# A gated recurrence and a spectral convolution on one core: odd batches walk the spectrum backwards, three kinds of operation may run on another engine, and the table of the order is new

## The chip, the core and the metric

The kernel runs on one core of a Trainium2 chip. The metric is the device time of one execution in microseconds (us). The median of three runs before the change is 484.12 us (484.09 to 484.51).

A core has engines that run side by side, each through its own list of instructions in order: TensorE (PE) multiplies matrices and writes them to PSUM; VectorE (DVE), ScalarE (ACT) and GpSimd (POOL) do elementwise work; SyncE (SP) here only issues DMAs, and all DMAs of this kernel are issued by it, in order. "PEld" in the profile is the load of a matmul's weights.

## What is computed

```python
# x, f_logit: (4, 6272, 256); B = 4 batches, S = 6272 steps, D = 256 channels
sig = 1.0 / (1.0 + np.exp(-f_logit))
f = lower_bound[None, None, :] + (1.0 - lower_bound[None, None, :]) * sig
i = 1.0 - f
for t in range(S):
    h = f[:, t] * h + i[:, t] * x[:, t]
    y[:, t] = h
...
proj = y @ w_proj                      # (4, 6272, 768) = x1, x2, x3
X2 = np.fft.rfft(x2, n=S, axis=1)
H = np.fft.rfft(filter_fft, n=S, axis=0)[None, :, :]
x2_conv = np.fft.irfft(X2 * H, n=S, axis=1)
out = (x1 * x2_conv * x3) @ w_out
```

The FFTs are done as products with matrices of cosines and sines. S is split as 128 x 49.

## The kernel before, in words

**Order.** Nothing of the order is decided while the kernel runs. The Python code first lists all operations with `op(kind, cost, fn, ...)`; `cost` names the engines on which an operation may run, with a price each that was used to make a plan, and `r` and `w` name what it reads and writes. `Plan.emit` (line 100) then issues them in the order of the string `ORDER` (line 117): three characters are 18 bits, the operation's number, its engine (ACT, DVE, PE, POOL or SP) and, for work in PSUM, the first of its banks. So the string fixes each engine's order, SyncE's DMAs among it, and the engine of each operation that has a choice. Many choices have `either` (line 282), ScalarE or VectorE.

**Stages.** `prepare` (line 395) makes the tables of cosines and sines and turns the filter once into its spectrum H, written to DRAM in 16 units of 8 pairs of channels. Then for each batch:
- `hgrn(b)` (line 299), 13 chunks of 512 steps: load f_logit into FL and x into XT (three buffers each, line 308); sigmoid (`sig`, ScalarE, line 311); the product of input and sigmoid (`u`, GpSimd, line 313); PE turns both (`su`, line 325); the gate's value (`f`, lines 338 and 340); VectorE's scan (line 346) writes h into HA; for the first 3072 steps a copy is wrapped behind the end of HA (`wrap`).
- `spectrum(b)` (line 764): `phase_p` multiplies h by the middle third of w_proj (`P`, line 673, 13 groups, cast to X2 by `x2`). Then for four groups of four units: `F1` (line 686) and its cast `A`; the small `mini` (line 702) with VectorE's `zm` (line 708). For each unit, `unit(b, u)` (line 717) loads the unit's part of H into one of three buffers Hu (`H`, line 721, one DMA of 392 KB), transforms (`F2`, line 731), has VectorE multiply by H (`prod`, line 744), and transforms back (`I2`, line 754, evicted to Th by `Th`).
- `gate(b)` (line 360), 13 chunks x 2 halves: x1 and x3 (`x13`, line 373) are evicted to x1s and x3s (`xs`), and their product goes to zt (`z`, GpSimd, line 389).
- `phase_o(b)` (line 774), 13 groups: the last inverse transform (`I1`, line 787), VectorE's product with zt (`y`, line 793), the projection with w_out (`proj`, line 805), the eviction into one of three osb buffers (`o`), and the store (line 815).

The order mixes these: hgrn of batch b+1 runs beside spectrum, gate and phase_o of batch b, and P of b+1 starts before phase_o of b is done. Copies go through a helper, so L270 and L272 are ScalarE's copies of many operations, L275 and L277 VectorE's, L280 GpSimd's; they are told apart by the tiles they write.

**Buffers of H.** Unit u of batch b takes the Hu buffer (16 b + u) modulo 3, whatever is in it; each of the 64 units has its own load, and a load waits until the products of the unit that held its buffer are done.

Of the kernel before, what the change touches and what calls it, by code (L numbers as in the profile page):

```python
# [58 lines left out]
class Plan:  # L59
# [58 lines left out]
    "A8gAAYBBgAOYABIAoQBLgACIBGgAmRBVgBQgAcSBagBfgAnTA7YAPIAyUBkgA9AAlVBpgBCAA+WBugBDQBAGAjSA/GBMYA6TBFABzgAgUBHY"  # L118
    "A5VBEIAQABNWERgA2SBPOA1TARIAvUBWAAYYB4gBIQAsVBRABXSADgAtUBOGBSUBYCAfWBbYESgBKAAxXArWBJABgYAeXBZCEdgBcQA3WBlA"
    "BTMBhSEpgApXBdIBqYBUEBmWATIBjCEegAUIBoGBvYBrUBeIBtEBiKAzQAFgBnGB0YBwQBsMAiSByABxIEqgB1WASAAGgAwTB5YETAB3OB9Y"  # L120
    "B6UA0SB2OAbQB7MAkRB8MCKSCIWAEYEUYCLCCBQEfACJOB/UAWICCICNSCAECEWCOKEVQCFGEgYEZUEWIAdSErAE1gAqTEXIE2gAhWEaECTS"
    "AIAAVYEbMEhWAHACDYElQAJAEsYEiOCUCCRUFBgEmAFCgEjOClSCSECQgCGgANACWUEnIE3ACMYEtWCVYCXEEuOExQE4YEvOFNgCmCCcUFOg"
    "EyACZgCaSCdMFDACjWEzIE5UCbCCkGE9SCeYE6MFEYALACfQFZgE+CE7MAuWFagAMACsWCPgAKACHgCgICuUCtGFPAFFWE/KFJQFGGFQYFjg"
    "CvEFHOCoSFkgFKAC3UChgCYgFbACpKA4WCnYFRWC4EFLIFcYCxSFSGFVUCyCFTOC1QFtgFugFWEC+SCqgEwYC2AFdWFXMCrgFlAE0YC6QCwY"
    "C5YC/CDAUC7IFmYFeGFgSDBEFfODJQFhCF3gC9gDHUDKAF4gFiKAXYFnWFvACigEcYDDQDCYFoODIEFqSFwYDEADSUFpOGBgGCgFrCDQQCzg"
    "DTEDMWC0gFsKDRADFgFMYFxUF5AC8gE8YDbQDNODLYFyEDZSDUYFAYDcADGgDVWFzMF6YDaCF0QDWGDiSF1IGLgDkUGMgDjKGDADeWEYYF2I"
    "DtSDlEDdYDYgGEYDfGDrUDOgF7QDsEDnWDuCF8IF+UDoGF9IEoYD0SGVgDmYF/EFYYD2WDqgDPgD1CDwQAaYGAMGWgD3GD/SDpgGNADxIGFW"
    "DhgDvYD5UGOYGGGEAKGIQD6EGHOD9SMVgGJADXgEIUD8gD+CEGWD4YGKIFIYEJEGPSEkYEHGGSUGXAGQKEBYECQEKYGTEMhgGYYGRKEPWD7g"
    "EDAAZYMWgMigGUMEQGGZSELQFUYGfgEFgGaCGcWJSUEEgGbKB+YGdGMXAJTVGeOJUMGgSEMAJVNGmWJWYGhCEOgDygGiUMtgMjAMugGsQDgg"
    "GnGGqSGtIDzgG0WGrCGwQHEgGjEENgGoSG1GGyUGpCGuWGzMGxAG2SGvGGkQG3KMvAG4UJXWGlAG5MJYXJcSJZGJdTJaHHLgG6QJfLG8UHSg"  # L130
    "JbYG7AJeKG+WJhTG9MG/GJgYHFQJiSJjDHHIHAWJkCJmUHBGHIIJlYJnVHMSJoEHCWJrQHPKHZgJpFJsRJtAJqYHiUJuBHOKJwQJxTJvYJyA"
    "J1RHDOHqgHjEJ2SJzLJ6QHGYJ3BHgWJ4KJ0YHJUHhGHTRHUYHKEHNYHkWJ5YHVJJ7TJ8AJ/UHlGHWJHQQJ9DHaVHRAKBMHxgJ+YHrSHcNKAX"
    "HmQHbYKCHMwYHdNHXUHnAKEXHYEHuKHeQH4gKGHIGUKDYHtKHfAHoWKFTIHEHyQHpOH/gKJSKHDH0IHsYIIUKLCKIYHvWIJEH1IH5SHzYHwG"
    "IKUH6YMYYH7KIQgH2QILEIAWH8KH3AIMUKKSINEICOIXgH9QKMCKOTIDOKPUH+AKNYKTVKQDIOQIegIRWKREIPIIBYKUSKVFKSYITOIsTKWC"
    "IEQItDIUOISYIYVIZYKXYIFAKYSIaNIlgKZUKaCKdTIuQIbNKfDKeXIvAIVSKbMI2gIfVKgHKcYIWCImQIiNKiUIcSIgYKkEKhYIhNKjXIdC"
    "KnWIpIKlHIjUI9gKpGKmYI3SIkEIoIIwWInYKoRIxGMkYI5KIqUJEgKqBKsQI6KKtWIrEI+RKvGMZUKrYJLgJAJKuAMdWMaEKxTKwYM5gMeG"
    "MbMKyQM6gKzDK2RK0AJBJIyTK4BK1YIzDMlQMfOK3VMcYMmAMpSK5FMnII0WMqCNFgMxUK6YNGgM7AI1OK7QMrKK8RI/YMyEI4YM1WM8YK+B"
    "MzMK9ANRgI7SM2GNSgLARI8CM3OLBQJGYJFULCBK/YLFSLDAJHMNHAM9WLEYNBQJIMM+GJCTNdgLHCNIYNegM/ONCALGVLKSNTANDIJMWLIF"
    "NUYJDDLLVJOONJQLMCLNFLPTJPONKANNUNfALJYNngNLINVWNogNOELQSLOYLRDNPMNZQNWGNgYRVTLSCNxgNXONaAJJUNygRXDRWSJKENbI"
    "LTYNhWRYCNkTNpANiOJNYJQQN8gNjONlDN7gNqYRaVJRARbSNmLRdCLUWRcFLZQLVONQYNrSNuUNsCLaILWWOFgNzAOGgNtKLbQNvEN0YLXG"  # L140
    "NwMLjSN9ALeWLYgLkKM0YLcAN1UN+YLfOLoSN2ELdgN4QN3MLgWN5AOPgOQgOHAMgYN6ILlULhGOIYLpKLtQLmELigN/WLuIOCSOAGLqUMsY"
    "OZgODCOBONMYOagLngNAYLyQLrEOEKNYYOJWORAOMULsgLzILvSUYgONEOSYOKGOOML0QObALwCOLOL3UMoAOcYLxgOTSM4YL4MOWWOUCL1A"
    "UkgOVKL8UPVgNEAOdQL2gOXGL9ML5SOeANcAOfIL+UL6COYOOgQL/EMGSL7gOhIUxgMBWOiIUwgMLUMCOUZgOvQMAgMHKPOgMDWOwAPHgOpS"
    "MEGOnQOqKOzWOoAO3SO0GOlQO4COtWOmAOrSOuOO5QOsCOxWO6IUyAO1SOyGMMMOjQO2CO7WMIUOkAO8OMNSUmAMJMMQQMOCO9WMRIO/UO+O"
    "RZYPBQPAEPDSPCIPIWReYPECPPUUaAPKOPFQRfSUzYRgTRhCPGIRkWRiDPLOPjQRmGPlSPkAPJYRlWRjYPSMPcgRpXRnGMFgPMQPmCPQYPRM"
    "RoYPWVRrHPdSPYNPtgPNARqUPXYRuXRsEPZNPTQRwHRtYPpUPUAPfKPnWP0gPeYPqEPaQUbYPgKPoGPuURvSP7gPbAPwMRzTUlgPrWRxCPhQ"
    "R1DPsOR0SPxMPvYP1TRyYR2CQJWPiAP4LQCgR4SQKGPyQP3LP8UR6CP9YP2YQLWPzAR3YP+MQTgP5SQMGQDQP/MP6CQNWR5UQGIQOGQagQAS"
    "R7ER9VQFIQUWQBCR8YR+RR/FQWOQhgQPSSABQEYSCUQQCSBYQHQQXOQbVQIAQRSSDXQogQdNSEESHQSFHSIRSJAQSKSGYUcUSKBQeNQvSUdE"
    "SMXQVYQwCQcYUeMQxQSLYQ5gSNWSOHQYSQyISPGQiUQZCSQYQzWQkMSRQQ0GSSRQlMQfSSUBQpWSTAQqYRAgQgCQ1USVYQsOUgQQ2ESWSQjY"
    "QrOU9gUnYUhASXTQmUSZDUiIRHgSYCQtWU8gQnEQ3SQ6QSaYQ4KQuGRBUQ8ISbSRCYScTSdCSgWRDMSeDShXSiGUoSSfYREMSjHSlQUpCSmU"  # L150
    "SkYQ9ISnASqWSoESrXQ7YRIUU+AUqKSpYROgQ+QMPgSsGStPU/YRFSQ/ARLMUsWRGCSvQVIgRKMUtGRPRVJgSxASuYSwVUuOS0TSyFS1QRJY"
    "S2DSzYU0URSJS3AS5WU1ES6XRQYRRJS4YS7GU4SS8HS+QVUgU2MS9YVKARTWVVgS/RRUGU5KRMUVLYTBJTAATDWRNEU6KVAQTEXVBATFOVEU"
    "TCYTGHVCITISVFEVhgVMWVggTHYVWAVGMMKgVQQTJTVNGVqgVXYTKKMSUTLDVOOVRATNSMTETOTTPCMUgTSUVSITMYTQDVYVVrgXRgTTXVZF"
    "TXSTRYTVPTUEVcQVaNViATWYZYXV0gZZUV1gVdAVjYZdVTYKZeWZaHZgGZfNTZSVsAVeITcWTaCTdOThQVtYZbEVkSTbgVnUTiIVlCTeWV+g"
    "VoEV/gVmKVuQTfGVpMTmSV2ATggVxWTnKWJgTjUVvAV3YWIgVyGVwITrSTkEVzOWAATlgV4QV7UV5ATsKWBYToWWSgUjAV8EV6ITtSTpGV9M"
    "T1QUvYTuCTqgTwWVPYWTgUfAT2IWCSTvgU3YVbAWFUU7YWDCTxOT3QWcgWKAWdgWEKTyWWGEWLYWUAWHMT6STzGT7KT/UVTYT4AWMWUAMWPS"
    "WVYWNGT5gT8QWQCT0gWOOUEUT9AWRKVHYWWWWeAVfYWZQWXGUFMWfYUBScogWaAVDYcbgUrAWYOXYgUGUUCCccgT+gWbIWgWWjScngWhGUHE"
    "czgWiOUDgUJQWkKUOWWlKUKIW+UXKgW4SW/EUPOW0Qc0gW5CULUW1AW8WcdAWoSW9OWyQWpCWsWUMEWwSWtOWzAW2UcpAWuQW3EcqYW6WWvA"
    "WmUW7OWxCWqQWnMUQWWrAUTSURGXAUUUKXCQZhYXBMXESXDAXGWZcYXFKXLUXHGXSQceYc1AXOMXISZiWZjXZkGXJKZnVZlHXVIXmSZpFXMY"
    "XoWXnCZmYZoVXNMZsRZqFcfSXTYZuBXUIZrYXfgcjUcgCZtRc/gXpGchKZxQXwgdAgckEZyWZvJcrSZzAclMZ0GXWQcsCZ1YXsWXXActKXgU"  # L160
    "ZwYXZQXtGXjMcvSXhYdBAXPWc2YXiMZ2VcwCXQGXcIZ3UX+gdLgZ4FXqWUIgcxKZ5EZ7RXrGZ8VZ6YaAUXbIaBSZ9BXkWXaYaDCZ+NX3gaCE"
    "XdQdMgXlGZ/YXuSX4UXvKXeAYOWX5YXxSdCYYPGYMQX0Kc3WYNAXzKaFTc4GaEYc7QaHDX6MYFgaGSc8AaKTaICX7MaLUaMDaJYaPSaNEaQT"
    "c9IdNAYWgX8UXyYdYgaOYdXgX9EaSLX1Qc5OaRCdOYX/TX2AaUVYBLaVSaWFYQWaXCYGQYCLaTYYRGYSSaZVYIIYTCYdgaYYaaWaeXabFafU"
    "YJIYHYacGdDSYAYc6YahEYUVajQdECYkgYVNadYakRagHdFKYKUdZAYDWYfYaiYamJalAYXSYEGaoRYZKanYYLEYyWapQYzGYaKYeUYYYatS"
    "arAYgMYbWYrgaqBavCY0QasYYhMYcGYlTauSY1AYmYYoLYiWY8gawCY2QYjGYtYYnLaxYYsUY3AaySYuMY4WZDgdaYa0CYpQUSgY5GUNgYvM"
    "Y9ScmAY6WazUZAKYqAZKga3Va1EYwQY7Oa2YZETY/KYxAdHWa5FY+Ya4QZHLZRgdIGZBRdkga6Aa8VdjgdJOZCBZMYa9Ua7YbBQa+FZLRZGL"
    "a/EZFYZSWbDAbAYbCVZOJfNgZITbEFbGQZNJbFYZJDbHVbLSbIAZVObMTZTYbJFdPQbNCbKYdTUZUObODbQXdQAdtgciYZPSbSHdugdRIbPY"
    "dlAUVWdUMZQCZWQdmYUWOcuAbRSdVMUXgdbWbTCZXAbVTdcOdfUbUYbXDbWSddOdgEd3ghbQd4gbYChcRdhMbaSbZYheBbfWhdAc+YbbKdvA"
    "dnUdqQdoEdwYbgOhgSeBgdrAhhTeCghiCdpMbcWd5AdsIhjDbkUd6YbdGdxSblMd0QdyCbegbhWdSAeLgdzKeMgd1Ad7UbiGd2IbpSeDAd+W"
    "bjgbqKbmQeWgd8EeEYeVgd/Gd9MbrSbnAeAObsCbuUbogcyYeFQfUgeNAbvMbzSeIWeOYb0KeJGefgbwUbtgeGAeKOb4SbxEeHIdWAePWdGA"  # L170
    "b1Ub5KeQGb9QeXAeROeSSb2EeYYb+Ib6WeTCb3gehAbygeUKdKAcCUeggb7GdeYeZQcDMdiYecSeaAb8gcHWedCebIb/UeeKcEQcAEeiYcIO"
    "cFAcMScBgejUcNKemQcJWenAekMcOSeoIcKGelMcRQcPCcWUe9WcXMcSIcQgepSfbge+GhkYezUeqKfBQexWhfYfCIevSeyGe7Qe0EetWe8A"
    "e3UeuGe5QewCe1We6Ae/Se4EerQfAKe2GhlUhmVesAhqWhoNhrXhnEhsOfDShtHhpYfFQfECfHUfGIfJWhuYfIEfOShvQfKGfRKhwRfVUhyB"
    "fQKfLWh0ThxAh1RhzYh2DfMOh5Qfigh3Bh6SfXMfpWh4Yh7Ah+TfqGfYMfrQfPYh/Uh8CfSWiALfzgiBEh9YiDVcGgfsAfcScLgfWYiEUfTG"
    "ffKiCYftQiGEfZWiFFfeKfjTfuAiHYiIVfmLf6gfaGiJSfdYfvQfkYiKFflLfgWfwAiNUfhOiOViLCgBgf0QiPEiMYiQFfxSiSWfyKgPUf2I"
# [11 lines left out]
def kernel(  # L187
# [79 lines left out]
    def copy(e, dst, src, scale=None):  # L267
# [5 lines left out]
        elif e == "DVE":  # L273
            if scale is None:
                nc.vector.tensor_copy(dst, src)  # L275
            else:
                nc.vector.tensor_scalar(dst, in0=src, scalar1=scale, scalar2=None,  # L277
                                        op0=AOP.mult)
        else:
            nc.gpsimd.tensor_copy(dst, src)  # L280

    def either(n, runs=1.0):

        return {"ACT": 0.045 + runs * n / 1200.0, "DVE": 0.07 + n / 960.0}
# [429 lines left out]

    def unit(b, u):
        ka = u % NA * UE
        k = (b * NU + u) % NP
        h = (b * NU + u) % NH  # L720
# [156 lines left out]
```

## Time and profile before

| what | value |
|---|---|
| median of three runs | 484.12 us |
| the profiled execution: time, span | 487.22 us, 485.2 us |
| mean granted clock of TensorE | 0.993 |
| busy: PE, ACT, DVE, POOL | 451.7, 423.0, 413.3, 299.6 us |
| moved by DMA | 116.49 MB, 240 GB/s on average |
| H loads (line 721) | 64 of 392 KB |
| z on POOL (line 389) | 104, 1214 ns each |
| u on POOL (line 313) | 52, 2247 ns each |
| H product on DVE (line 744) | 128, 1199 ns each |
| scan on DVE (line 346) | 104, 123.1 us in all |

The profiled execution has a span (first to last instruction) and a time that includes what lies around it. A row of the profile's groups reads: line, engine, operation, what is written <- what is read, shapes, count | busy us, mean ns of one | idle time of the engine just ahead of these instructions, and what ended that idle time. The chain of waits is followed back from the last instruction, at each step to what released it or to the instruction before it on its engine. In a timeline each row is a start, a length, an engine and an instruction; in SyncE's rows the length of a merged row includes what it waited for.

Batch 0's P begins at 77.5 us of the span, and P of batch 3 at 397.7 us; the four changes of stage are at about 77, 180, 290 and 398 us.

### The profile page before, as it was taken

What the parts mean: (1) busy time and instruction counts of PE and PEld (TensorE: products, weight loads), DVE (VectorE), ACT (ScalarE), POOL (GpSimd) and SP (SyncE); (2) the same over time, 40 slices, a digit from 0 to 9 for tenths busy, and PEclk for the clock granted to TensorE, in tenths of its full rate; (3) what the DMA queues carried; (4) which work ended last, traced back from release to release, by engine and by line L of the source; (5) the groups of instructions that cost most, each with busy time, mean ns of one, the idle gap of its engine ahead of it and who ended that gap; (6) DMA issues with size and microseconds to landing.
All of it is one profiled execution on the core that took longest, in us unless ns stands there. A gap on an engine that the chain in (4) does not pass through costs nothing.

```text
span 485.2 us, 14710 instructions
## 1 busy us (share of the span) xinstructions
PE 451.7 (93%) x6041; PEld 347.1 (72%) x6041; DVE 413.3 (85%) x446; ACT 423.0 (87%) x613; POOL 299.6 (62%) x313
## 2 busy tenths in 40 slices
PE   8988998999999989999998998989989899999995
PEld 7776777677667879767566888656757788676784
DVE  7788985899999985999999984979989984999773
ACT  6988999999998969989898978999979868999844
POOL 6775994486897910946896723878675522666600
PEclk9999999999999999999999999999999999999998
DMA  8989999545688994464879975475777861544177
GB/s 330 397 287 354 329 306 313 188 122 162 208 274 291 356 346 173 134 195 135 240 236 360 386 265 228 152 232 190 227 245 250 315 227 38 178 148 151 54 287 294
DMA packets 41731, 116.49 MB, mean 240 GB/s; under 512 B 4384, under 2 KB 6304, under 8 KB 41664
## 3 DMA queue, kind: packets, MB, share of 16 engines
q1 hardware_dynamic: 41664, 115.56, 70.0%
q8 instruction: 47, 0.77, 0.7%
q14 instruction: 20, 0.16, 0.1%
HBM read 84.54 MB, written 31.00 MB: 238 GB/s over the span
## 4 chain that ended last, share of the span: by engine, by line
PE 46%; DMA 17%; DVE 14%; ACT 10%; issue 5%; POOL 3%; SPq 1%; ACTq 0%; DVEq 0%; POOLq 0%
PE PS L373 11%; DMA out_dram<-osb 8%; PE PS L673 7%; DMA FL<-in_f_logit_dram 6%; PE PS L754 6%; DVE PP L744 5%; PE PS L805 5%; DVE HA L346 5%; PE PS L731 4%; PE PS L686 4%; PE PS L325 4%; DMA Hu<-H 2%; ACT osb L272 2%; ACT fTs L338 2%; PE PS L787 2%
## 5 line engine op out<-in xcount | busy, mean ns | idle before, releaser
L389 POOL TENSOR_TENSOR zt<-x1s,x3s 128x490 f16<-128x490 f32 (+1 forms) x104 | 125.3, 1214 | 94.5 <-ACT x3s L270 43.9
L744 DVE TENSOR_TENSOR PP<-PS,Hu 98x1008 f16<-98x1008 f32 x128 | 146.5, 1199 | 8.6 <-PE PS L731 3.3
L313 POOL TENSOR_TENSOR XT<-XT,FL 128x1024 f32<-128x1024 f32 (+1 forms) x52 | 116.8, 2247 | 47.5 <-ACT FL L311 18.6
L346 DVE TENSOR_TENSOR_SCAN HA<-fTs,HA,PS 128x512 f16<-128x512 f32 (+1 forms) x96 | 113.4, 1204 | 6.9 <-ACT fTs L338 5.9
L373 PE MATMUL PS<-HA,W 128*128 128x490 f16 (+1 forms) x416 | 105.5, 370 | 3.1 <-DVE PP L744 1.4
L793 DVE TENSOR_TENSOR ys<-PS,zt 128x1024 fp32r<-128x1024 f32 (+1 forms) x52 | 58.6, 1151 | 9.0 <-PE PS L787 3.6
L272 ACT ACTIVATE osb<-PS 128x1024 f32<-128x1024 f32 (+1 forms) x49 | 47.7, 988 | 19.6 <-PE PS L805 11.1
L338 ACT ACTIVATE fTs<-PS,nomc 128x512 f32<-128x512 f32 (+1 forms) x89 | 59.3, 680 | 4.6 <-PE PS L325 4.1
L270 ACT CAST HA<-PS 128x1024 f16<-128x1024 f32 x57 | 57.8, 1032 | 3.8 <-PE PS L686 3.3
L805 PE MATMUL PS<-Wo,ys 128*128 128x256 f32 x392 | 56.8, 291 | 3.2 <-ACT osb L272 1.7
L311 ACT ACTIVATE FL<-FL 128x1024 f32<-128x1024 f32 (+1 forms) x52 | 53.1, 1021 | 7.6 <-DMA FL<-in_f_logit_dram 7.4
L272 ACT ACTIVATE x1s<-PS 128x490 f32<-128x490 f32 (+1 forms) x95 | 56.0, 592 | 3.5 <-PE PS L373 1.3
L373 PEld LDWEIGHTS <-W 128*128 128x128 f16 x416 | 33.9, 98 | 33.7 <-issue 10.8
L754 PEld LDWEIGHTS <-PP 98*128 98x128 f16 x1024 | 49.5, 98 | 11.9 <-issue 3.3
L270 ACT COPY x3s<-PS 128x490 f32<-128x490 f32 (+1 forms) x90 | 51.8, 579 | 4.6 <-PE PS L373 3.1
L805 PEld LDWEIGHTS PS<-Wo,ys 128*128 128x128 f32 x392 | 49.0, 188 | 7.9 <-ACT osb L272 2.2
L325 PE MATMUL PS<-iden,FL 64*128 64x64 f32 x784 | 46.6, 233 | 7.8 <-ACT afs L270 2.1
L754 PE MATMUL PS<-VA,PP 98*128 98x98 f16 x512 | 51.8, 207 | 1.6 <-DVE HA L346 0.9
L270 ACT CAST Th<-PS 128x784 f16<-128x784 f32 x62 | 50.9, 830 | 1.4 <-PE PS L754 1.2
L325 PEld LDWEIGHTS PS<-iden,FL 64*128 64x128 f32 x784 | 34.0, 139 | 25.2 <-DVE HA L346 5.6
L754 PE MATMUL PS<-VB,PP 98*128 98x98 f16 x512 | 51.6, 207 | 0.0
L673 PE MATMUL PS<-W,HA 128*128 128x256 f16 x392 | 44.8, 273 | 3.4 <-ACT osb L272 3.4
(110 smaller groups left out, 677.9 us busy)
## 6 DMA issues: line engine op xcount, KB each, us to landing
Hu<-H SPq DMA_DIRECT2D x64, 392.0 KB
FL<-in_f_logit_dram SPq DMA_DIRECT2D x48, 512.0 KB
XT<-in_x_dram SPq DMA_DIRECT2D x48, 512.0 KB
out_dram<-osb SPq DMA_DIRECT2D x48, 512.0 KB
X<-in_moe_filter_fft_dram SPq DMA_DIRECT2D x9, 512.0 KB
H<-Hu SPq DMA_DIRECT2D x16, 196.0 KB
H<-Hu SPq DMA_DIRECT2D x16, 128.0 KB
Hu<-in_moe_filter_fft_dram SPq DMA_DIRECT2D x2, 512.0 KB
```

The source lines that it names most:

```text
L270: nc.scalar.copy(dst, src)
L272: nc.scalar.activation(dst, src, AF.Copy, scale=scale)
L313: op("u", {"POOL": 0.1 + 0.553 * nb}, lambda e, xt=xt, ft=ft: nc.gpsimd.tensor_tensor(xt, xt, ft, op=AOP.mult), r=[("ft", k)], w=[("xt", k)])
L325: nc.tensor.transpose(bank(pb)[:, at[p] + j:at[p] + hn:nb], src[ps, j, cols], iden[ps, ps])
L338: nc.scalar.activation(fT, sT, AF.Identity, scale=by, bias=1.0)
L346: nc.vector.tensor_tensor_scan(h, fT, bank(pb)[:, 512 - hn:512 + hn], init, op0=AOP.mult, op1=AOP.add),
L373: nc.tensor.matmul(PS[:, p, 0:n], W13[:, kh, js], HA[:, HB[kh] + t0:HB[kh] + t0 + n], start=(kh == 0), stop=(kh == 1))
L389: nc.gpsimd.tensor_tensor(late["zt"][:, jb, :, m0:m0 + nm], xs(0), xs(1), op=AOP.mult),
L673: nc.tensor.matmul(pp[:, r - r0, :], column(HB[kh], q_of(r)), W2[:, kh, :], start=(kh == 0), stop=(kh == 1))
L744: nc.vector.tensor_tensor(PP[:TB, k, o, :, :, 1:64], px.unsqueeze(1).broadcast_to([TB, 2, UE, 63]), hh[:, :, :, 1:64], op=AOP.mult)
L754: nc.tensor.matmul(PS[:, ib + o, pr * TB:(pr + 1) * TB], PP[:TB, k, o, n, 2 * pr:2 * pr + 2, :], v[:TB], start=(n == 0), stop=(n == 1))
L805: nc.tensor.matmul(po[:, i, :], late["ys"][:, yk, kh, i * 128:(i + 1) * 128], Wo[:, kh, :], start=(kh == 0), stop=(kh == 1))
```

## The change

- The 16 units of H are walked from 15 down to 0 in batches 1 and 3 (the groups of four backwards too), and from 0 up in 0 and 2.
- `unit` keeps a list of which unit each Hu buffer holds. If the unit that is due is held, no load is listed; otherwise the buffer used longest ago is loaded. The PP buffer is counted by order of use.
- `u`, `wrap` and `z` have VectorE as a further choice (`either_of`).
- `ORDER` is a new string, made for the new list of 2325 operations (2334 before).

```diff
+    def either_of(e):
+
+        return nc.gpsimd if e == "POOL" else nc.vector
...
-            op("u", {"POOL": 0.1 + 0.553 * nb}, lambda e, xt=xt, ft=ft: nc.gpsimd.tensor_tensor(
+            op("u", {"POOL": 0.1 + 0.553 * nb, "DVE": 0.06 + 0.267 * nb}, lambda e, xt=xt, ft=ft: either_of(e).tensor_tensor(
                 xt, xt, ft, op=AOP.mult), r=[("ft", k)], w=[("xt", k)])
...
-                op("wrap", {"POOL": 0.05 + (z - t0) / 1015.0, "ACT": 0.08 + (z - t0) / 1200.0},
+                op("wrap", {"POOL": 0.05 + (z - t0) / 1015.0, "ACT": 0.08 + (z - t0) / 1200.0,
+                            "DVE": 0.07 + (z - t0) / 960.0},
...
-                op("z", {"POOL": 0.06 + 2.3 * n / 1000}, lambda e, xs=xs, jb=jb, m0=m0, nm=nm:
-                   nc.gpsimd.tensor_tensor(
+                op("z", {"POOL": 0.06 + 2.3 * n / 1000, "DVE": 0.07 + n / 960.0},
+                   lambda e, xs=xs, jb=jb, m0=m0, nm=nm: either_of(e).tensor_tensor(
                        late["zt"][:, jb, :, m0:m0 + nm],
                        xs(0), xs(1), op=AOP.mult),
...
+    held, recent = [None] * NH, list(range(NH))
+
+    def spectrum_load(u, h):
+        first = count["h"] < NH
+        count["h"] += 1
+        held[h] = u
+        op("H", {"SP": 0.46}, lambda e: nc.sync.dma_start(
+            Hu[:TB, h].rearrange("p a e k -> p a (e k)"), twice(H[u][:])),
+           r=[("H", u, i) for i in range(2)],
+           w=[("Hu", h)] + ([("hs", h, a) for a in range(2)] if first else []),
+           dma=1.7, lag=2.0, margin=MARGIN)
+
     def unit(b, u):
         ka = u % NA * UE
-        k = (b * NU + u) % NP
-        h = (b * NU + u) % NH
-        op("H", {"SP": 0.46}, lambda e: nc.sync.dma_start(
-            Hu[:TB, h].rearrange("p a e k -> p a (e k)"), twice(H[u][:])),
...
+        k = count["u"] % NP
+        count["u"] += 1
+        h = held.index(u) if u in held else recent[0]
+        recent.remove(h)
+        recent.append(h)
+        if held[h] != u:
+            spectrum_load(u, h)
...
-        for q in range(NU // NA):
-            for u in range(q * NA, q * NA + NA):
+        way = 1 if b % 2 == 0 else -1
+        for q in range(NU // NA)[::way]:
+            for u in range(q * NA, q * NA + NA)[::way]:
                 phase_f1(b, u)
             mini(b, q)
-            for u in range(q * NA, q * NA + NA):
+            for u in range(q * NA, q * NA + NA)[::way]:
                 unit(b, u)
```

The strings of `ORDER`, which differ nearly throughout, are left out.

## The prediction

> **What bounds the kernel now.** I read the page first, then busy time by stage, then the chain of waits and SyncE's queue around each change of batch. The page, engines and chain:
>
> ```profile
> PE 451.7 (93%) x6041; PEld 347.1 (72%) x6041; DVE 413.3 (85%) x446; ACT 423.0 (87%) x613; POOL 299.6 (62%) x313
> ...
> PE 46%; DMA 17%; DVE 14%; ACT 10%; issue 5%; POOL 3%; SPq 1%; ACTq 0%; DVEq 0%; POOLq 0%
> ```
>
> PE leads, but only 33.5 us of 485.2 are without a matmul, and this is the most that any edit can win without removing matmuls; the change removes none. DMA is the second share of the chain. Where those 33.5 us lie is in the busy times by stage (columns: stretch, length, then busy us of PE, PEld, DVE, ACT, POOL with counts, clock, DMA share, GB/s):
>
> ```profile
> 130.00:150.00 20.00, 18.64 (x289) 12.34 (x288) 19.91 (x20) 19.94 (x35) 18.39 (x16) 1.00 0.85 270
> ...
> 177.00:182.00 5.00, 4.05 (x42) 3.77 (x37) 3.31 (x3) 1.30 (x2) 0.00 (x0) 1.00 1.02 406
> ...
> 265.00:272.00 7.00, 5.80 (x102) 4.85 (x103) 6.67 (x7) 6.43 (x10) 5.64 (x4) 1.00 1.03 416
> ...
> 415.00:435.00 20.00, 20.00 (x275) 14.16 (x272) 18.63 (x21) 19.14 (x31) 13.84 (x18) 1.00 0.58 183
> ```
>
> In the middle of a batch (415 to 435) PE is full and DMA half idle. At a change of batch (177 to 182, 265 to 272; also 165 to 172, share 1.00 at 384 GB/s) DMA is full and PE loses up to a fifth of a stretch. Between (130 to 150) VectorE and ScalarE are full. The chain of waits says what the full DMA holds up:
>
> ```profile
> 172.72 8.89 DMA out_dram<-osb
> 181.71 1.03 ACT osb L272
> 182.79 8.24 PE PS L673 x74
> ...
> 284.58 9.19 DMA out_dram<-osb
> 293.79 1.03 ACT osb L272
> 294.87 4.71 PE PS L673 x40
> ```
>
> A store of the old batch takes 8.9 and 9.2 us to land (and 8.5 from 378.02, at the third change). The third-next eviction needs its buffer (three osb buffers), that eviction frees a PSUM bank, and the projection P of the next batch waits for the bank: the waits give PE L673 <- ACT osb 3.4 us in two waits, 1.7 at the first change of batch and 1.6 at the second. What shares the DMA queue with these stores is in SyncE's timeline:
>
> ```profile
> 171.43 0.34 SPq L308 DMA_DIRECT2D FL<-in_f_logit_dram  x1
> 171.87 0.65 SPq L721 DMA_DIRECT2D Hu<-H  x1
> 172.72 3.13 SPq L815 DMA_DIRECT2D out_dram<-osb  x2
> ```
>
> A spectrum load (392 KB) goes out just ahead of the store that the chain follows; so also at 283.68 before 284.58, and at 378.46, 0.4 us behind 378.02.
>
> **The change, part by part.** The table is words of operation, engine and bank, and its counts can be read off. Its old form gives what the profile counts (37 x2 casts on ScalarE and 15 on VectorE, 104 z on GpSimd), so I trust the reading of the new one.
>
> *Fewer spectrum loads.* With odd batches walked from unit 15 down, a batch begins with the three units that the one before left in Hu. Batches 1 to 3 load 13 instead of 16: 55 loads instead of 64, nine DMAs gone with their nine issues on SyncE (0.31 us each, and the waits ahead of them). One is 401 kB; at the 384 to 416 GB/s of the full stretches it costs the queue 1.0 us. All nine were the prefetches issued at the changes of batch, three at each. The loads that stay (from a batch's fourth unit on) wait for the first unit's products as before.
>
> First change of batch: in the old SyncE order, two loads (f of batch 2 and unit 2's spectrum) stand between stores 5 and 6; in the new one store 6 follows store 5 directly. That is 0.51 + 0.40 MB less ahead of it, about 2.4 us at 384 GB/s. The eviction that needs store 6 (group 9) also moves from behind the second P to behind the eighth, some 5 us of PE work later (98 matmuls of P in 10.9 us, 0.89 us for a group of eight). I take the whole wait of 1.7 us off. Second: the evictions of groups 10 and 11 move behind all thirteen P groups; store 7 now stands behind more (five loads and store 8, about 3.1 MB, 8 us), but 10.9 us of P cover that. I take the 1.6 us off; without the cover it would come back as about 2 us. Third: no store moves against its loads; only the load at 378.46 and the one at 352.84, behind an f load that took 9.12 us to land, leave. Between 0 and 2 us; I take 1.0, since PE was idle 1.8 of the 9 us from 378. Sum -4.3 us.
>
> *VectorE may take z, u and wrap.* No wrap does. Seven of 104 z and two of 52 u move; so do two of the filter's casts. GpSimd sheds 7 x 1.21 + 2 x 2.25 + 2 x 0.97 = 15 us, which is worth nothing by itself at 62% busy. No row has z on VectorE. The nearest are its two products of the same type with both inputs in SBUF:
>
> ```profile
> 7.49 0.70 DVE L476 TENSOR_TENSOR PP<-HA,PP 128x520 f32<-128x520 f32 x1
> ...
> 14.11 1.23 POOL L280 CAST afs<-X 128x1024 fp32r<-128x1024 f32 x1 [0.95 <-ACT f L270]
> 14.47 1.41 DVE L476 TENSOR_TENSOR PP<-HA,PP 128x512 f32<-128x512 f32 x1
> ```
>
> Alone 0.70 us, beside a GpSimd instruction 1.41. So z costs VectorE 0.67 alone (0.70 x 490/520) and 1.35 beside GpSimd; u is 1.21 (the ys row of 1024 elements) to 1.9. Here the Trainium skill speaks against the change: "SBUF — State Buffer", section "Who interferes with whom", holds that a VectorE instruction with two SBUF inputs and a GpSimd instruction that reads SBUF exclude each other for the whole instruction. By the order, two z of batch 3 find GpSimd free; five z and two u stand next to a GpSimd product. By the row these seven cost 7 x 0.71 = 5.0 us of delay; by the rule up to a whole GpSimd z (1.23, the median) or u (2.37) each, 5 x 1.23 + 2 x 2.37 = 10.9 us. I take the row, since the second product, too, started after the GpSimd instruction and lost only what was left of it. Behind each waiting product stand scans and spectrum products, for which PE's I2 waits. In batches 2 and 3 VectorE has 1 to 2 us free in 20, so I put 2.2 of the 5.0 us on the path (bounds 0 and 5). The last z of batch 3 is now split between the two engines: GpSimd ended its pair at 459.35, and y of group 0 waited 2.77 us for it, but the last Th (458.62) and I1 are due just before, and in the new order that Th (0.97 on VectorE for 0.83) and z stand on VectorE ahead of y. I value it at nothing (bounds -0.3, +1).
>
> *Other engine choices in the table.* Against the old one VectorE takes 7 x2 casts, 3 f, 1 Th, 1 o more and 4 f2, 2 hw, 1 xs fewer: 8.5 + 2.2 + 1.0 + 1.3 - 2.8 - 2.4 - 0.7 = +7 us; with z, u and the casts +16 us on 413. ScalarE loses 7 x 1.05 + 3 x 0.68 + 0.8 + 1.0 - 4 x 0.69 - 2 x 1.03 - 0.6 = 6 us. The x2 part is free: during P VectorE waits for PE (DVE X <- PE L673, 23.8 us), and that wait covers the 8.5 us. Without it, P would be slowed by 1.2 us a cast. The rest adds to VectorE before batch 0, where DMA holds the pace (share 0.92 to 0.98 to 77 us).
>
> *Order before batch 0.* All thirteen filter loads now go out before the first f load; two x loads of batch 1 fall behind spectrum loads. The bytes needed before 77 us stay. Between -1.5 and +1; I take -0.5, as FF1 waited 0.6 us for the filter's last piece at 23.9. Elsewhere neighbours swap places; I see no reason for a sign and count 0, +-2.
>
> Sum: -4.3 + 2.2 + 0 - 0.5 = -2.6 us. The profiled execution took 487.2 us (span 485.2 and 2.0 around it), 3.1 over the median of the runs, 484.1; the difference is 0.5% and carries over: 484.1 - 2.6 = 481.5.
>
> **Rivals.**
> *Slower: the exclusion of VectorE and GpSimd.* If the rule's price holds (10.9 us) and three quarters are on the path because VectorE is full (19.91 of 20 at 130 to 150), the sum is -4.8 + 8.2 = +3.4, 487.5 us. It decides from 4.8 us on the path. Against it: only about one product in batch 0, one or two in 1 and 2 each, and the most in batch 3, where PE has been the full engine.
> *No change: the wait moves.* In 150 to 172 VectorE is busy 21.85 of 22; P begins after the last scan, and if the scans are late, the stores' earlier landing only shows as another wait. Then 4.3 shrinks to 2 and contention takes it: 484.1.
> *All of it.* PE is idle about 10 us at the three changes (2.0 in 172 to 195, 4.2 in 260 to 300, 4.1 in 360 to 400). If the nine loads (9 us of queue) win two thirds and contention is hidden: 484.1 - 6 = 478.
>
> **How the numbers follow.** Forecast (-1 to -4.5 us) 0.42, all of it 0.12, no change 0.13, slower 0.33: a table with this many swaps can lose in places that I haven't priced, and I put that beside the exclusion. A measurement can tell about 0.2%, 1 us, from no change. Faster 0.54, same 0.13, slower 0.33. The range takes in the rival at 487.5 and the one at 478: 477.5 to 488.
>
> **What would show it.** 55 loads at L721, none between the last stores of one batch and P of the next; PE L673 <- ACT osb falls from 3.4 us to under 1; DMA legs of out_dram in the chain become fewer or under 7 us; L744's idle time and L793's wait for z don't rise by over 2 us; z on VectorE reads 0.7 alone and up to 1.4 beside GpSimd (1.9 would be the rule's price). PE's busy time stays at 452 and its idle time falls to about 31. Wrong would be: PE's gaps at the changes of batch kept under another releaser, or VectorE's products of about 2 us with gaps of PE behind them.

## The result, and the profile after

| | before | changed |
|---|---|---|
| median | 484.11 us (4 runs, 482.25 to 484.51) | 478.69 us (4 runs, 477.76 to 479.30) |
| ratio of the two | | 0.9894, 95% interval 0.9864 to 0.9924 |
| profiled execution: time, span | 487.22, 485.2 us | 478.75, 476.7 us |

The change saves 5.4 us by the medians. Medians and ratios here and below are of fast executions alone, without three slow ones: one of 12 of the kernel mid_new (488.64 us) and two of 12 of late_new (487.77 and 2308.47 us).

The two profiled executions differ by 8.5 us, as the one of before was 3.1 us over its median. Its TensorE clock was granted at 0.83 between 360 and 370 us (at 0.50 for 3.4 us of them), which accounts for up to 1.7 of the 3.1. In the table below, the stretch that holds this place (batch 2 to 3) took 2.9 to 3.3 us more in before than in two other kernels with the old order, loads_only and evict_only; these will serve there.

The page of the changed kernel, engines and chain:

```profile
PE 447.1 (94%) x6041; PEld 345.1 (72%) x6041; DVE 431.8 (91%) x462; ACT 415.8 (87%) x608; POOL 286.4 (60%) x302
...
PE 52%; DVE 19%; ACT 11%; DMA 7%; issue 6%; POOL 2%; SPq 1%; ACTq 0%; DVEq 0%; POOLq 0%
```

DMA's share of the chain fell from 17% to 7%; PE's rose from 46% to 52% and VectorE's from 14% to 19%. VectorE's work grew by 18.5 us, close to the 16 that the table's counts gave. The waits on stores, first of before, then of the changed kernel (us in all, times, longest):

```profile
ACT osb L272 <- DMA out_dram<-osb: 7.5, 9, 2.4
...
PE PS L673 <- ACT osb L272: 3.4, 2, 1.7
```

```profile
ACT osb L272 <- DMA out_dram<-osb: 2.6, 4, 1.2
```

P's own wait for an osb eviction (3.4 us, in the row of PE above) is gone from the changed kernel's list, as forecast. It would be easy to stop here and call the gain explained. The experiments say that this is the smaller part.

A word on marks. The start and the end of P don't contain the same work in both orders, as projections have moved past it. Better marks are the first spectrum product (VectorE, PP<-PS,Hu) of one batch and the first of the next, as every order has the same 128 of them. Work of other stages can move across these marks, too, so a gain in one column has to be seen with its neighbours. The profiles give, in us:

| kernel | start to batch 0 | batch 0 to 1 | 1 to 2 | 2 to 3 | 3 to the end | span |
|---|---|---|---|---|---|---|
| before | 92.6 | 103.5 | 107.6 | 109.0 | 72.6 | 485.2 |
| changed | 95.0 | 101.3 | 103.6 | 103.8 | 73.0 | 476.7 |
| loads_only | 92.5 | 103.0 | 107.5 | 106.1 | 73.0 | 482.0 |
| evict_only | 93.7 | 102.6 | 107.9 | 105.7 | 72.7 | 482.7 |
| loads_back | 96.3 | 101.6 | 105.1 | 104.1 | 73.4 | 480.6 |
| products_back | 94.6 | 101.6 | 103.4 | 103.6 | 73.4 | 476.5 |
| mid_new | 94.1 | 103.7 | 104.6 | 107.9 | 72.4 | 482.6 |
| late_new | 93.4 | 103.1 | 109.3 | 104.1 | 72.5 | 482.4 |
| old_start | 95.9 | 101.4 | 103.6 | 103.1 | 73.5 | 477.4 |

The first two columns together change by 0.2 us between before and changed. The gain is in the next two columns, the two cycles between the first products of batches 1, 2 and 3: 4.0 us in the first of them, and 1.9 to 2.3 in the second if it is taken against evict_only and loads_only (5.2 against before, with its slow clock).

A cycle has a middle, from the first to the last spectrum product of its batch, and a change to the next batch behind it. In no profile was the clock below full in the middles of batches 1 and 2. In us, by the order that the kernel has in that stretch:

| middle of | old order | new order |
|---|---|---|
| batch 1 | before 46.9, loads_only 46.8, evict_only 47.6, late_new 46.8 | changed 44.8, loads_back 45.1, products_back 45.2, mid_new 45.2, old_start 44.8 |
| batch 2 | before 53.8, loads_only 54.3, evict_only 53.1, mid_new 55.6 | changed 51.9, loads_back 51.6, products_back 51.6, late_new 51.1, old_start 51.1 |

### The profile page after: what moved, and what is told of

It reads as the page before. It is cut to its first block, busy times and chain, and to the rows that moved or that the text cites. A ratio compares the mean times of both kernels' runs of the same rounds, so it can differ in the third digit from the quotient of the medians.

```text
span 476.7 us, 14696 instructions
## 1 busy us (share of the span) xinstructions
PE 447.1 (94%) x6041; PEld 345.1 (72%) x6041; DVE 431.8 (91%) x462; ACT 415.8 (87%) x608; POOL 286.4 (60%) x302
## 4 chain that ended last, share of the span: by engine, by line
PE 52%; DVE 19%; ACT 11%; DMA 7%; issue 6%; POOL 2%; SPq 1%; ACTq 0%; DVEq 0%; POOLq 0%
PE PS L378 13%; DVE HA L350 9%; PE PS L773 8%; PE PS L678 6%; PE PS L750 6%; DVE ys L813 5%; PE PS L691 5%; PE PS L825 4%; PE PS L329 4%; DMA out_dram<-osb 2%; DMA H<-Hu 2%; PE PS L620 2%; DVE PP L763 2%; DMA X<-in_moe_filter_fft_dram 2%; ACT fTs L342 2%
## 5 line engine op out<-in xcount | busy, mean ns | idle before, releaser
L394 POOL TENSOR_TENSOR zt<-x1s,x3s 128x490 f16<-128x490 f32 (+1 forms) x97 | 117.6, 1218 | 69.7 <-ACT x3s L270 53.0
L317 POOL TENSOR_TENSOR XT<-XT,FL 128x1024 f32<-128x1024 f32 (+1 forms) x50 | 112.0, 2244 | 57.8 <-ACT FL L315 53.2
L825 PE MATMUL PS<-Wo,ys 128*128 128x256 f32 x392 | 58.2, 293 | 4.3 <-DVE ys L813 3.2
L342 ACT ACTIVATE fTs<-PS,nomc 128x512 f32<-128x512 f32 (+1 forms) x86 | 56.6, 672 | 5.1 <-PE PS L329 4.4
L272 ACT ACTIVATE x1s<-PS 128x490 f32<-128x490 f32 (+1 forms) x93 | 54.4, 588 | 7.1 <-PE PS L378 3.4
L272 ACT ACTIVATE osb<-PS 128x1024 f32<-128x1024 f32 (+1 forms) x48 | 46.3, 974 | 14.7 <-PE PS L825 11.5
L270 ACT COPY x3s<-PS 128x490 f32<-128x490 f32 (+1 forms) x93 | 53.3, 576 | 3.5 <-PE PS L378 2.5
L315 ACT ACTIVATE FL<-FL 128x1024 f32<-128x1024 f32 (+1 forms) x52 | 53.1, 1025 | 0.1
L773 PE MATMUL PS<-VB,PP 98*128 98x98 f16 x512 | 51.6, 207 | 0.0
L329 PE MATMUL PS<-iden,FL 64*128 64x64 f32 x784 | 44.9, 231 | 6.2 <-DVE HA L350 1.9
```

The costliest lines, as they stand in the source:

```text
L270: nc.scalar.copy(dst, src)
L272: nc.scalar.activation(dst, src, AF.Copy, scale=scale)
L317: op("u", {"POOL": 0.1 + 0.553 * nb, "DVE": 0.06 + 0.267 * nb}, lambda e, xt=xt, ft=ft: either_of(e).tensor_tensor(xt, xt, ft, op=AOP.mult ...
L329: nc.tensor.transpose(bank(pb)[:, at[p] + j:at[p] + hn:nb], src[ps, j, cols], iden[ps, ps])
L394: lambda e, xs=xs, jb=jb, m0=m0, nm=nm: either_of(e).tensor_tensor(late["zt"][:, jb, :, m0:m0 + nm], xs(0), xs(1), op=AOP.mult),
L773: nc.tensor.matmul(PS[:, ib + o, pr * TB:(pr + 1) * TB], PP[:TB, k, o, n, 2 * pr:2 * pr + 2, :], v[:TB], start=(n == 0), stop=(n == 1))
```

## The experiments

Two theories stood against each other. The prediction's was that the nine loads and the place of the evictions free the store that P waits for. The rival was that the gain is in the new order elsewhere, and the loads give little. A third question was what the products on VectorE cost.

**The nine loads alone.** The new operations with the old order and the old engines; the units of odd batches are relabelled, and nine words are dropped from the table.

```diff
  ... store 0.5  loadf 2.1
- H 1.2
  store 0.6  store 0.7  loadx 2.2  loadf 2.2  loadx 2.0  store 0.8
- H 1.1  H 1.0
  ... (likewise H 2.0 to 2.2 and H 3.0 to 3.2)
```

> The old order and the old engines, but odd batches walk backwards and the nine loads are gone. If the nine loads carry the gain (they shared the full DMA with the stores for which the next batch's P waits), this takes off 3 to 4 us: ratio 0.992 to 0.994, and P's wait for osb falls from 3.4 us to about 1.5, since only at the first and third change do loads stand before or beside the stores that decide. If the gain is the new order's, this is within 1 us of before (0.998 to 1.002), and the wait for osb stays over 2.5 us.

482.44 us, ratio 0.9972 (0.9944 to 0.9999), about 1.4 us. That lies between the two expectations: less than half of what the loads were given, and with an interval that all but reaches 1. ScalarE's wait for stores fell from 7.5 to 4.1 us. In its profile the cycle from batch 1 to 2 didn't move (107.5), though the clock was granted at 0.50 from 278.5 to 281.9 us there, which can hide up to 1.7 us.

**The nine loads put back into the changed kernel.** The table has nine more words where the order of before had its loads.

```diff
-        if held[h] != u:
+        if held[h] != u or b and (u > 12 if b % 2 else u < 3):
             spectrum_load(u, h)
```

> The changed kernel, with the nine loads put back where the kernel before had them: the three units that Hu still holds are loaded once more at each change of batch. If the loads carry the gain, 3 to 4 us come back and it lies at 481.5 to 483 (ratio to before 0.995 to 0.998). If the new order hides the stores behind P whatever the loads do, it stays within 1 us of the changed kernel (0.988 to 0.991).

480.1 us, ratio 0.9941 (0.9914 to 0.9968) against 0.9894 for the changed kernel: again between the two expectations. 1.4 us came back by the medians, 2.3 by the ratios (the two intervals just overlap). From the other side it is about the same price. ScalarE waits for the stores as long as before the change:

```profile
ACT osb L270 <- DMA out_dram<-osb: 7.5, 9, 1.8
```

So with all 64 loads, and with ScalarE's waits on stores as long as in before, this kernel is still 4.0 us by the medians and 0.6% by the ratio faster than before (0.3% to 0.9%). Neither the loads nor these waits can be where most of the gain came from.

**The place of the evictions alone.** The kernel before with all its loads; only the projections and evictions that the chain showed are moved behind P groups, and the PSUM banks within P are dealt out anew.

```diff
- P 1.6  proj 0.9  P 1.3  o 0.9  P 1.2  P 1.8 ...
+ P 1.6  P 1.3  P 1.2  P 1.8  P 1.10  P 1.1  proj 0.9  P 1.5  P 1.4  o 0.9 ...
- P 2.12  P 2.9  P 2.7  proj 1.10  P 2.11  P 2.1  P 2.6  P 2.3  o 1.10 ...
+ P 2.12  P 2.9  P 2.7  P 2.11  P 2.1  P 2.6 ... P 2.2  proj 1.10  o 1.10
```

> The kernel before with one thing moved: at the first change of batch the projection and eviction of group 9 stand behind the sixth and eighth group of P, at the second those of group 10 behind the last group. All 64 loads stay. If the place of these evictions is what took away P's wait for osb, the 3.4 us of that wait go and the time falls by 2 to 3 us (0.993 to 0.996). If the loads must go too, because the projection only waits later, it is within 1 us of before.

484.83 us, ratio 1.0025 (0.9991 to 1.0059): no gain, or at most 0.4 us of one. Yet P's wait did go, and ScalarE's wait for stores fell from 7.5 to 3.5 us. The rows of P's matmuls at the first two changes of batch, from its first to its last start, are in before:

```profile
L673 PE MATMUL PS<-W,HA x98: 269/272/330, 177.2 to 190.8; 128*128 128x256 f16 x98
...
L673 PE MATMUL PS<-W,HA x98: 269/273/330, 285.5 to 299.3; 128*128 128x256 f16 x98
```

and in evict_only:

```profile
L671 PE MATMUL PS<-W,HA x98: 270/273/330, 179.2 to 191.0; 128*128 128x256 f16 x98
...
L671 PE MATMUL PS<-W,HA x98: 270/273/329, 286.0 to 297.1; 128*128 128x256 f16 x98
```

P shrank from 13.6 to 11.8 us and from 13.8 to 11.1, 4.5 us in all. But the two cycles that hold these changes took 102.6 and 107.9 us against 103.5 and 107.6, 0.6 us less together. At the second change the wait only moved: F1 (line 684 of this kernel), which follows P, now waits for the eviction, as long as P did.

```profile
PE PS L684 <- ACT osb L270: 1.5, 1, 1.5
```

At the first change, where the projection and its eviction stay inside P, no such wait came up, and P ended its work in 1.8 us less. The cycle was 0.9 us shorter, which one profile can't tell from noise; where the rest went stays open. What the 12 executions say is that 3.4 us of P's waiting, taken away alone, were worth at most 0.4 us.

**The products on VectorE put back.** Nine words change their engine from DVE to POOL; two casts of the filter stay on VectorE.

```diff
- z 1.11.1 DVE   z 2.5.0 DVE   z 3.0.0 DVE ... u 0.0 DVE   u 3.0 DVE
+ z 1.11.1 POOL  z 2.5.0 POOL  z 3.0.0 POOL ... u 0.0 POOL  u 3.0 POOL
```

> The changed kernel with its seven z and two u that run on VectorE put back on GpSimd, all else in place. The prediction's step says they cost 2.2 us on the path: then this is faster than the changed kernel by 1 to 3 us (ratio to before 0.983 to 0.987). The rival says that they help, as a z of 0.66 us instead of 1.22 lets y of the last batch begin sooner and u frees FL and XT sooner: then it is slower by 0.5 to 2 us (0.990 to 0.994).

478.22 us, ratio 0.9890 (0.9854 to 0.9927): no difference from the changed kernel (0.9894), and neither expectation. VectorE's busy time fell by 8.2 us (431.8 to 423.6), GpSimd's rose by 12.6, and the time stayed; no stretch of the table moved by more than 0.4 us. The intervals, 1.5 and 1.8 us to either side, leave room for a small cost or for a cost and a gain that cancel. What z costs on VectorE is in one row of the changed kernel (ns: least, median, most):

```profile
L394 DVE TENSOR_TENSOR zt<-x1s,x3s x7: 646/659/1422, 250.3 to 449.6; 128x490 f16<-128x490 f32 x6, 128x392 f16<-128x392 f32 x1
```

0.66 us alone against 0.67 forecast. The exclusion shows where GpSimd's instruction is under way already:

```profile
291.59 2.39 POOL L317 TENSOR_TENSOR XT<-XT,FL 128x1024 f32<-128x1024 f32 x1 [10.68 <-ACT FL L315]
292.46 2.61 DVE L317 TENSOR_TENSOR XT<-XT,FL 128x1024 f32<-128x1024 f32 x1
...
449.56 1.02 POOL L394 TENSOR_TENSOR zt<-x1s,x3s 128x392 f16<-128x392 f32 x1 [2.29 <-ACT x3s L270]
449.58 1.42 DVE L394 TENSOR_TENSOR zt<-x1s,x3s 128x392 f16<-128x392 f32 x1
```

GpSimd's z ended at 450.58. VectorE's began 0.02 us after GpSimd's had begun and ended at 451.00, 0.42 us after GpSimd's end: so it seems to have waited for all of it, 1.00 us. The u, likewise, ended 1.09 us behind GpSimd's end at 293.98, after 1.52 us of waiting. This is what the Trainium skill states in "SBUF — State Buffer", section "Who interferes with whom": the port pair that the two share is an exclusive lock, and the loser is blocked until the other's instruction has ended. The row that I had preferred (0.71 us more) fits the same rule: GpSimd's instruction there had 0.87 us left when VectorE's began. But only three of the nine met such a neighbour. The third is the z at 250.28 with 1.07 us. Together they lost (1.07 - 0.66) + 1.00 + (2.61 - 1.22) = 2.8 us (1.22 is the other u, which met nobody), and putting all nine back brought nothing of it back that these runs can tell.

**The middle cycle in the new order.** The next two go behind the loads alone and replace one stretch of the order.

```diff
  (loads_only up to the last P of batch 1)
- the old order to the last P of batch 2
+ the new order to the last P of batch 2
  (loads_only from there)
```

> The kernel with nine loads fewer and the old order (loads_only), but from the end of the second batch's P to the end of the third's it follows the new order, engines included. In the profiles this stretch shrank from 108.5 to 102.5 us, and not in loads_only (108.4). If the new order of this stretch is what gains there, the time falls by 2.5 to 4.5 us below loads_only (ratio to before 0.988 to 0.992). If the profiled execution of before was only a slow one, or the gain is of the whole order, it stays within 1 us of loads_only (0.995 to 0.999).

482.86 us, ratio 0.9961 (0.9931 to 0.9991): 0.5 us below loads_only's ratio, and within its interval. The cycle itself did gain: 104.6 us against 107.5 (and 107.6 in before, at full clock). The next one lost: 107.9 against 106.1, 1.3 us of it in the middle of batch 2, whose order is the old one in both.

**The cycle after it in the new order.**

```diff
  (loads_only up to the last P of batch 2)
- the old order to the last P of batch 3
+ the new order to the last P of batch 3
  (loads_only from there)
```

> As mid_new, but the new order is followed from the end of the third batch's P to the end of the fourth's, and the old one elsewhere. Before took 109.0 us for it, loads_only 106.1, the changed kernel 105.6. If the loads alone gain here, this is within 1 us of loads_only (0.995 to 0.999); if the order does, 2 to 3 us less (0.991 to 0.993).

482.48 us, ratio 0.9966 (0.9938 to 0.9995): no gain over the loads alone. Again the cycle gained, 104.1 against 106.1, and its neighbour, this time the one before, took 109.3 against 107.5. In both profiles a cycle beside the new stretch took 1.8 us more. That the place where an old and a new stretch meet costs this is my reading, from one profile each; the two times do say that neither stretch carries the gain by itself.

**The old start.**

```diff
- the new order up to the last P of batch 0
+ the old order up to the last P of batch 0
  (the changed kernel from there)
```

> The old order up to the end of the first batch's P (tables, filter, first recurrence), and the changed kernel's order from there. In the profiles P of the first batch begins at 77.3 us before and at 78.5 in the changed kernel. If the new start is worse, as these say, the time falls by about 1 us below the changed kernel (ratio to before 0.986 to 0.988) and this is the best version; the prediction gave the new start 0.5 us of gain, and then it rises to 479.2 or more (0.990 or more).

478.93 us, ratio 0.9874 (0.9837 to 0.9912): the same as the changed kernel within both intervals. The ratio is one that was expected if the new start is worse, but the medians differ by 0.2 us the other way. The new start neither gains nor loses what can be measured, and the 1.2 us by which P of batch 0 begins later in the changed kernel's profile mean nothing: in six profiles of kernels with one and the same start, P begins anywhere from 77.2 to 78.9 us. This run also fixes where the gain is: behind P of batch 0, as far as an interval of 1.8 us to either side can tell.

It bears on the engines, too. Word by word, 128 operations have another engine in the new table than in the old one; most of them trade places, so the net counts of the prediction are much smaller. The old start puts 47 of them back, products_back nine (one of them among the 47), and neither changes the time.

## Why the prediction was right, point by point

The direction was right, and the time lies in the range; by its size it is the rival "all of it" (478), not the forecast (481.5), and that rival's reason, the loads, was wrong too. None of the four terms of its sum had the right size: too much gain from the loads and too much cost of the products about cancelled, and the gain of the order was missed. That the number came out in the range is luck, for the account behind it was largely wrong.

- *The loads and the stores, -4.3 us.* Measured: 1.4 us by loads_only, 1.4 to 2.3 by loads_back. The wait of P went, as the step said, but the step counted a wait in the chain as time. evict_only removed the same wait and gained nothing: of the 4.5 us by which P shrank, 0.6 were left at the next batch's first product, and 1.5 us of the wait had moved to F1. In that much the rival "the wait moves" was right.
- *Products on VectorE, +2.2 us.* Measured: nothing within the intervals. There were three collisions instead of seven, 2.8 us instead of 5.0, and none of it shows in the time: the largest, 1.39 us, fell at the change of batch at 292 us. The rule described a collision rightly. The rival built on it (487.5) named the right mechanism, but assumed a collision for every neighbour in the order; an order names neighbours, not instants.
- *The start, -0.5.* Measured: nothing, within 2 us.
- *"Elsewhere neighbours swap places; I see no reason for a sign and count 0, +-2."* This is the step that failed. About 3.5 us of the 5.4 are here: 5.4 less the 1.4 to 2.3 of the loads, with nothing from the products and the start, leaves 3 to 4. loads_back gives it directly, as the changed kernel with all the loads: 4.0 us by the medians, 2.9 by the ratio (1.5 to 4.2). That is outside the +-2 by its middle, though not by its whole interval.

Where this shows best is the table of the middles. In the nine profiles every middle of batch 1 or 2 with the new order is shorter than every one with the old, by some 2 us on the whole: with the loads or without, with the products on VectorE or not, and in mid_new and late_new with the old order around them. Here is the one of batch 2, before, then changed (columns as in the prediction):

```profile
303.60:357.40 53.80, 51.00 (x697) 34.20 (x696) 49.14 (x53) 50.70 (x81) 42.03 (x45) 1.00 0.67 212
```

```profile
299.80:351.70 51.90, 50.34 (x699) 33.78 (x695) 50.07 (x53) 48.65 (x78) 38.38 (x45) 1.00 0.64 202
```

The stretch is 1.9 us shorter while VectorE does 0.9 us more in it: its idle time falls from 4.7 to 1.8 us. Its releasers there were, before:

```profile
DVE zp L708 <- PE PS L702: 1.4, 1, 1.4
DVE PP L744 <- PE PS L754: 1.2, 1, 1.2
DVE PP L744 <- PE PS L731: 1.2, 2, 0.8
DVE PP L744 <- DMA Hu<-H: 0.5, 1, 0.5
```

and after:

```profile
DVE PP L763 <- ACT x1s L272: 0.7, 1, 0.7
DVE PP L763 <- PE PS L750: 0.7, 2, 0.4
DVE zp L713 <- ACT x1s L272: 0.2, 1, 0.2
```

PE's idle time falls from 2.8 to 1.6 us. The same stretch of batch 1 shrank from 46.9 to 44.8 us, with VectorE's idle time down from 3.1 to 1.4 and PE's from 1.6 to 0.3, while PE does 620 matmuls in it instead of 604. So in the middle of these batches no engine was full before. VectorE's products waited about a microsecond at a time for PE (in batch 1 the longest wait was one of 1.5 us for an eviction on ScalarE). PE waited for VectorE in turn (line 373 for the products, 1.4 us in batch 2 before). The new order takes some of these waits away. I had read 19.91 of 20 at 130 to 150 us as "VectorE is full" and the 415 to 435 stretch as "PE is full", and concluded that there was nothing to win in the middle. In batches 1 and 2 PE was busy 97% and 95% of the middle: I had shown the middle of batch 3, where no next recurrence competes and PE was never idle, for the middle of any.

Two claims behind the +7 us of other work on VectorE were not tried by themselves: that the seven casts of P are free there, and that ScalarE's 6 us less are worth nothing. What there is fits the first: four of the seven are in P of batch 0, old_start put them back, and that P took 10.7 us against 10.8; and in the changed kernel's third P VectorE was busy 7.9 of 10.7 us and PE all of it. I also put a filter cast on VectorE at 1.2 us; it took 0.69.

What stays open is which of the swaps make the middle faster. mid_new and late_new each win 2 to 3 us in their own cycle, and a neighbour's takes 1.8 more, so the gain isn't in one stretch alone; whether the two stretches together bring all of it was not run. That it lies in the order and not in an engine choice is inferred: mid_new and late_new carry 22 and 23 of the other engines along with their stretch of order, and these were never put back alone.

## What to carry to other kernels

A wait on the chain is worth its length only if the work behind it ends sooner: before counting it, take the next instruction that both versions must run (here the next batch's first product) and ask what else stands ahead of it. Compare stages between marks that every version has, with as nearly the same work between them as can be found, and look at each batch's own middle before calling an engine full. A new order couldn't be priced by its parts here: each replaced stretch won in its own cycle, and a neighbour's lost most of it. So put a new order as a whole beside one with a single thing undone, and leave a wide term for it in the sum.

## What the hardware showed that I had not expected

A cast of 1024 fp32 elements for each partition from SBUF to SBUF (to fp32r) took VectorE 0.69 us. A cast of as many from PSUM (to fp16) took it 1.22:

```profile
L275 DVE CAST afs<-Hu 128x1024 fp32r<-128x1024 f32 x1 | 0.7, 694 | 1.0 <-PE PS L595 1.0
...
L275 DVE CAST X<-PS 128x1024 f16<-128x1024 f32 x19 | 22.6, 1219 | 9.6 <-PE PS L678 9.5
```

And the profiled executions of one and the same first stretch differ by 1.7 us (77.2 to 78.9): a single profile settles no question of that size. The clock doesn't account for it. In five of the nine profiles it was granted at 0.50 for 3.4 us once on the way, at 42 us in late_new, 50 in old_start, 78 in loads_back, 279 in loads_only and 362 in before, which can cost up to 1.7 us each time; but of the six that share the start, the latest P (78.9, mid_new) began with no such stretch ahead of it.
